# Scores, maxima and sums in one ring of three PSUM tiles, sums inverted on 128 partitions, the last pair scaled among the first MLP units

## The chip, the cores and the metric

The kernel runs on one core of one Trainium2 chip. The metric is the time of one execution on the device in microseconds (us), the median of several runs. The engines that compute are TensorE (PE, with its weight loads as PEld), VectorE (DVE), ScalarE (ACT) and GpSimd (POOL). SyncE (SP) issues nearly all transfers.

## What is computed

```python
# attention: q is averaged over pairs of positions first; 2 batches, 8 heads, 1152 positions, head size 64
scores = 1/sqrt(64) * matmul(q_pool, k.T)            # per head 576 x 1152
attn = exp(scores - max(scores))                     # maximum over the 1152 keys
attn = attn / (sum(attn) + 1e-9)
x = matmul(attn, v)                                  # -> 1152 tokens x 512
# two MLP layers, 512 -> 2048 -> 512
h = x @ w_in;  g = h * tanh(softplus(h));  x = g @ w_out        # layer 0 (Mish)
h = x @ w_in2; g = h if h > 0 else exp(h) - 1; out = g @ w_out2  # layer 1 (ELU)
```

The MLP weights come as 64-bit floats. Each block of them is rebuilt as a 32-bit float from its two words.

## The kernel before

**Pairs and steps.** The heads are taken in 8 pairs (two heads fill the 128 partitions). A pair has two halves of queries, c = 0 (256 queries) and c = 1 (320). Each half has 9 steps, one for each block of 128 keys, so a pair has 18 steps. In every step TensorE makes the transposed scores of that block (`qk`, L308: three products of high and low parts, and L310: a product that adds the row `top` with the negated maxima), and ACT takes the exponential (`exp`, L316) into the tile `pt`.

**Maxima.** The maxima have to be known before a pair's scores. So 14 "peaks" of the next pair (numbered 0 to 13) are worked in between: a product of queries and keys into the tile `M` (`peak_mm`, L254; the last two, for the queries that don't fill a block, at L260), and a reduction on DVE (`peak`, L268, L270, L272) into `stat`. After peak 5 and after peak 13 the maxima are negated (L280, L282), written to DRAM (`hopm`) and read back as a row (`top`, L291 and L296). Peaks 0 to 5 of the next pair stand at steps 5 to 10, peaks 6 to 13 at steps 12 to 17 and at steps 0 and 1 of their own pair. For pair 0, peaks 0 to 5 stand ahead of the first step and peaks 6 to 13 at steps 0 to 7.

**Output products and sums.** The products with v (`av`, L364, into the tile `C`) follow in groups: for c = 0 five key blocks at step 11 and four at step 15; for c = 1 five at step 2 of the next pair and four at step 6. POOL adds up part of the exponentials (`add`, L329) and TensorE finishes the sums over keys with a product of ones (`total`, L339, tile `T`) behind the group of four. Then DVE adds 1e-9 and inverts (`invert`, L347, L348; four rows of up to 160 numbers, repeated on 32 partitions each), the result goes through DRAM (`hop`, L350) and comes back spread over partitions (`rb`, L353). ACT copies the product out of `C` (`keep`, L372), DVE scales it 9 steps after the inversion (`scale`, L387), ACT and DVE split it into the high and low parts of the tokens (`token_high` L392 into `XH`, `token_low` L397 into `XL`).

**PSUM.** The 8 banks are: `M` one tile of two banks, `S` (scores) two tiles of two banks, `T` one bank, `C` one bank.

**What sets the order.** The code is emitted step by step in a fixed order that the table `todo` holds; each engine works through its own instructions in that order. In a step the peak's product comes first, then the scores, then `av`, ACT's work, DVE's, POOL's and SP's. Each pair also reads one half block of MLP weights (`Weights`): read at step 5 (SP, L97), and by its age in steps rescaled on ACT (4, L109), clamped on POOL (5, L113), shifted and merged with its words on DVE (7 and 8, L118, L123, L124), and split (9 and 10, L132, L135).

**MLP.** 96 units (2 layers, 48 each), one after another: TensorE makes `h` of unit u (L168), and the output products of unit u - 3 (L588).

## Time and profile before

| | |
|---|---|
| median of 3 runs | 771.13 us (766.66 to 772.33) |
| profiled execution, time | 777.13 us |
| profiled execution, span of its trace | 775.3 us |
| PE busy | 678.2 us (87%) |
| DVE busy | 456.5 us (59%) |
| ACT busy | 341.5 us (44%) |
| POOL busy | 233.8 us (30%) |

The attention stage ends at about 361 us and the MLP units begin there. The profile shows for each instruction its start, its duration and what it waited for; a busy TensorE need not be one at its peak, since its matmuls are pipelined and their ends modelled. "Granted clock" is the clock of TensorE, 1.00 for 2.4 GHz and 0.50 for 1.2 GHz.

### The profile page before, as it was taken

The page shows a single profiled execution, that of the slowest core. Times are in us where ns is not written, and L with a number is a line of the kernel's source. Part 1 is how long each engine was busy: PE and PEld are TensorE (multiplying, and loading weights), DVE is VectorE, ACT ScalarE, POOL GpSimd, SP SyncE. Part 2 cuts the span into 40 slices and gives each one's busy share as a digit, 9 for nine tenths or more (in the row PEclk, how much of TensorE's full clock was granted, in tenths as well). Part 3 has the DMA queues.
Part 4 walks back from the last instruction along what each step waited for, and adds up shares of the span by engine and source line. Part 5 has one row for each costly group of instructions (what it writes and reads, how often), then busy time and mean ns, then how long its engine had stood idle before and what let it go on. Part 6 is the DMA issues. An engine that isn't in the chain of part 4 may idle for free.

```text
span 775.3 us, 11575 instructions
## 1 busy us (share of the span) xinstructions
PE 678.2 (87%) x4616; PEld 569.5 (73%) x4616; DVE 456.5 (59%) x700; ACT 341.5 (44%) x678; POOL 233.8 (30%) x213
## 2 busy tenths in 40 slices
PE   2677878787778688699799999999999999999997
PEld 1455545455555455466799999999999989989996
DVE  4444464546463634624754666667778777998543
ACT  1333334243434333342543444444466666665442
POOL 3443545455553525343110112323322000110000
PEclk9998888798979878799899999999999999999999
DMA  2221121212131301011422322222212222230111
GB/s 91 89 68 32 41 97 37 92 42 94 35 101 36 101 8 51 25 37 42 165 82 82 109 81 70 95 82 82 82 55 82 82 82 82 83 109 1 41 42 41
DMA packets 43592, 53.30 MB, mean 69 GB/s; under 512 B 14033, under 2 KB 34449, under 8 KB 43537
## 3 DMA queue, kind: packets, MB, share of 16 engines
q1 hardware_dynamic: 43024, 51.83, 21.4%
q8 instruction: 36, 0.59, 0.3%
q10 hardware_dynamic: 512, 0.72, 0.3%
q14 instruction: 20, 0.16, 0.1%
HBM read 50.11 MB, written 2.43 MB: 68 GB/s over the span
## 4 chain that ended last, share of the span: by engine, by line
PE 78%; DVE 14%; ACT 3%; DMA 3%; issue 2%; SPq 1%
PE A L168 25%; PE B L588 21%; PE C L364 12%; DVE stat L268 6%; PE S L308 6%; PE C L588 5%; PE M L254 4%; PE T L339 3%; DVE inv L348 2%; PE S L310 2%; DVE wf L124 2%; ACT pt L316 2%; DVE wf L123 1%; DMA top<-hopm 1%; DVE stat L270 1%
## 5 line engine op out<-in xcount | busy, mean ns | idle before, releaser
L316 ACT ACTIVATE pt<-S 128x512 f32<-128x512 f32 (+1 forms) x144 | 92.6, 651 | 211.5 <-PE S L310 211.4
L268 DVE TENSOR_REDUCE stat<-M 128x2 f32<-128x768 f32 x96 | 91.1, 949 | 107.1 <-PE M L254 107.1
L168 PE MATMUL A<-XH,wh 128*128 128x384 f32 x384 | 129.7, 338 | 6.5 <-ACT g L543 5.9
L113 POOL TENSOR_SCALAR wf<-wf 128x512 f32<-128x512 f32 x64 | 42.8, 669 | 294.5 <-ACT wf L109 261.2
L168 PE MATMUL A<-XH,wl 128*128 128x384 f32 x384 | 129.6, 338 | 0.0
L168 PE MATMUL A<-XL,wh 128*128 128x384 f32 x384 | 129.4, 337 | 0.0
L254 PE MATMUL M<-KH,QH 64*128 64x384 f32 x192 | 49.8, 508 | 67.3 <-DVE stat L268 61.1
L364 PE MATMUL C<-pt,vr 128*64 128x320 f32 (+1 forms) x576 | 96.1, 490 | 0.5 <-ACT x L372 0.5
L254 PEld LDWEIGHTS M<-KH,QH 64*128 64x128 f32 x192 | 21.6, 217 | 91.3 <-DVE stat L268 74.7
L329 POOL TENSOR_TENSOR add<-pt 128x512 f32<-128x512 f32 (+1 forms) x32 | 45.1, 1410 | 122.0 <-ACT pt L316 121.9
L168 PEld LDWEIGHTS A<-XH,wh 128*128 128x128 f32 x384 | 72.6, 189 | 9.0 <-ACT g L543 6.2
L329 POOL TENSOR_TENSOR add<-add,pt 128x512 f32<-128x512 f32 (+1 forms) x48 | 73.3, 1541 | 16.7 <-ACT pt L316 16.6
L364 PEld LDWEIGHTS C<-pt,vr 128*64 128x64 f32 x576 | 46.4, 166 | 39.0 <-issue 19.9
L168 PEld LDWEIGHTS A<-XL,wh 128*128 128x128 f32 x384 | 72.7, 189 | 1.9
L168 PEld LDWEIGHTS A<-XH,wl 128*128 128x128 f32 x384 | 72.6, 189 | 0.0
L542 ACT ACTIVATE gh<-A 128x384 fp32r<-128x384 f32 x48 | 23.7, 494 | 81.5 <-PE A L168 81.5
L310 PE MATMUL S<-top,unit 64*128 64x320 f32 (+1 forms) x288 | 51.4, 339 | 6.8 <-DMA top<-hopm 6.8
L124 DVE SCALAR_TENSOR_TENSOR wf<-raw,wf 128x512 int32<-128x512 int32 x64 | 54.1, 845 | 2.2
L308 PE MATMUL S<-QH,KH 64*128 64x320 f32 (+1 forms) x288 | 53.5, 363 | 1.0 <-ACT pt L316 0.7
L545 DVE TENSOR_TENSOR gl<-g,gh 128x384 fp32r<-128x384 f32 x48 | 32.0, 668 | 35.8 <-ACT g L543 35.7
L588 PE MATMUL B<-gh,wh 128*128 128x384 f32 x155 | 52.3, 337 | 0.0
L588 PE MATMUL B<-gh,wl 128*128 128x384 f32 x155 | 52.2, 337 | 0.0
(88 smaller groups left out, 1369.7 us busy)
## 6 DMA issues: line engine op xcount, KB each, us to landing
raw<-in_moe_w_in_dram SPq DMA_DIRECT2D x32, 512.0 KB
raw<-in_moe_w_out_dram SPq DMA_DIRECT2D x32, 512.0 KB
vr<-in_v_dram SPq DMA_DIRECT2D x8, 576.0 KB
qr<-in_q_dram SPq DMA_DIRECT2D x7, 576.0 KB
kr<-in_k_dram SPq DMA_DIRECT2D x7, 576.0 KB
out_dram<-part SPq DMA_DIRECT2D x8, 256.0 KB
rb<-hop SPq DMA_DIRECT2D x16, 80.0 KB
rb<-hop SPq DMA_DIRECT2D x16, 64.0 KB
```

What stands on the lines that cost most here:

```text
L113: nc.gpsimd.tensor_scalar(self.f, self.f, HUGE, -HUGE, op0=ALU.min, op1=ALU.max)
L124: nc.vector.scalar_tensor_tensor(f, self.low, 29, f, op0=ALU.logical_shift_right, op1=ALU.bitwise_or)
L168: nc.tensor.matmul(pt[:, :TB], w[:, kk * P:(kk + 1) * P], x[:, kk, tk], start=(i == 0), stop=(i == len(terms) - 1))
L254: nc.tensor.matmul(pt[:, h, :KB], qh[n][half[h], t * P:(t + 1) * P], kh[n][half[h], j * KB:(j + 1) * KB], start=True, stop=True,)
L268: nc.vector.tensor_reduce(m[:, t, :, j], pt[:, :, :KB], axis=AX.X, op=ALU.max)
L308: nc.tensor.matmul(pt[:, h, :w], x[half[h], kk], y[half[h], cols], start=(i == 0), stop=False)
L310: nc.tensor.matmul(pt[:, h, :w], unit[half[h], :], tops[n % 2][half[h], cols], start=False, stop=True)
L316: nc.scalar.activation(pts[n, c][:, kt], sc.pop((n, c, kt))[:, :, :w], AF.Exp, scale=SCALE)
L329: nc.gpsimd.tensor_tensor(d, d if i is None else p[:, i], p[:, j], op=ALU.add)
L364: nc.tensor.matmul(acc[n, c][half[h], :w], vs[n][:, h, kt, :], pts[n, c][:, kt, h, :], start=(kt == 0), stop=(kt == KT - 1),)
L545: nc.vector.tensor_tensor(gl, g, gh, op=ALU.subtract)
L588: nc.tensor.matmul(pt, l, r, start=(first and i == 0), stop=(final and i == 2))
```

## The change

Five edits:

- **One ring.** Peaks, scores and sums take their PSUM tiles from one ring `S` of three tiles of two banks, in the order in which they are emitted. `C` gets two tiles instead of one, so that the output products can stay in PSUM until they are scaled.
- **Sums.** ACT copies the sums out of the ring (`spill`, one step after `total`); they go to DRAM and come back as one number or a few for each of 128 partitions (`tot`, 4 or 5 wide). DVE inverts these (`invert`, 4 steps after the copy), and they go to DRAM again (`pop`) and come back spread out (`rb`). `scale` follows 4 steps after `invert` (9 before), and reads the output products from `C`; the copy `keep` is left only for the last pair.
- **Last pair.** Its `invert`, `scale`, `token_high` and `token_low` stand in MLP units 1 to 7.
- **Weights** in the attention stage are read at step 12 instead of 5, so that their DVE work falls on steps 1, 2 and 4 of the next pair.
- **Pair 0.** Peaks 6 to 9 stand ahead of the first step too; 10 to 13 stand at steps 0 to 3.

```diff
-                pt = sc[n, e] = ps.tile([P, 2, 512], F32, tag="M", name="M", bufs=1)
+                pt = sc[n, e] = ps.tile([P, 2, 512], F32, tag="S", name="M", bufs=3)
...
-                pt = sc[n, c, kt] = ps.tile([P, 2, 512], F32, tag="S", name="S", bufs=2)
+                pt = sc[n, c, kt] = ps.tile([P, 2, 512], F32, tag="S", name="S", bufs=3)
...
-                pt = sums_[n, c] = ps.tile([P, 512], F32, tag="T", name="T", bufs=1)
+                pt = sums_[n, c] = ps.tile([P, 2, 512], F32, tag="S", name="T", bufs=3)[:, 0]
...
+            def by_four(hop):
+                return hop.rearrange("(g p) a -> g (p a)", g=4)
+
+            def spill(n, c):
+                w = cut[c][1] - cut[c][0]
+                r = ap.tile([P, 5 * D // 2], F32, tag="sum", name="sum")
+                nc.scalar.copy(r[:, :w // 2], sums_.pop((n, c))[:, :w // 2])
+                hop = dp.tile([P, w // D], F32, tag=f"hop{c}", name="hop")
+                nc.sync.dma_start(out=by_four(hop), in_=r.rearrange("(g p) w -> g p w", p=32)[:, 0, :w // 2])
+                pool, bufs = home(n)
+                r = tots[n, c] = pool.tile([P, w // D], F32, tag=f"tot{c}", name="tot", bufs=bufs)
+                nc.sync.dma_start(out=r, in_=hop)
+
             def invert(n, c):
-                w = (cut[c][1] - cut[c][0]) // 2
-                r = ap.tile([P, 5 * D // 2], F32, tag="inv", name="inv")
-                nc.vector.tensor_scalar(r[:, :w], sums_.pop((n, c))[:, :w], 1e-9, None, op0=ALU.add)
-                nc.vector.reciprocal(r[:, :w], r[:, :w])
-                hop = dp.tile([4, 5 * D // 2], F32, tag="hop", name="hop")
-                nc.sync.dma_start(out=hop[:, :w], in_=r.rearrange("(g p) w -> g p w", p=32)[:, 0, :w])
+                w = cut[c][1] - cut[c][0]
+                r = tots.pop((n, c))
+                nc.vector.tensor_scalar(r, r, 1e-9, None, op0=ALU.add)
+                nc.vector.reciprocal(r, r)
+                hop = dp.tile([P, w // D], F32, tag=f"pop{c}", name="pop")
+                nc.sync.dma_start(out=hop, in_=r)
...
-                    acc[n, c] = ps.tile([P, 512], F32, tag="C", name="C", bufs=1)
+                    acc[n, c] = ps.tile([P, 512], F32, tag="C", name="C", bufs=2)
...
             def scale(n, c):
-                rb, x = xs[n, c]["rb"], xs[n, c]["x"]
                 w = cut[c][1] - cut[c][0]
-                nc.vector.tensor_tensor(x[:, :w], x[:, :w], rb[:, :w], op=ALU.mult)
+                pool, bufs = home(n)
+                x = xs[n, c] = pool.tile([P, w], F32, tag=f"y{c}", name="y", bufs=1)
+                nc.vector.tensor_tensor(x, acc.pop((n, c))[:, :w], rbs.pop((n, c)), op=ALU.mult)
...
-                    at(u0 + KT + 6, "av", total, n, c)
-                    at(u0 + KT + 7, "dve", invert, n, c)
-                    at(u0 + KT + 7, "act", keep, n, c)
-                    at(u0 + KT + 16, "dve", scale, n, c)
-                    at(u0 + KT + 17, "act", token_high, n, c)
-                    at(u0 + KT + 18, "dve", token_low, n, c)
+                    t0 = u0 + KT + 6
+                    at(t0, "av", total, n, c)
+                    at(t0 + 1, "act", spill, n, c)
+                    if n < n_pairs - 1:
+                        at(t0 + 5, "dve", invert, n, c)
+                        at(t0 + 9, "dve", scale, n, c)
+                        at(t0 + 10, "act", token_high, n, c)
+                        at(t0 + 12, "dve", token_low, n, c)
+                    else:
+                        at(t0 + 1, "act", keep, n, c)
+                        for u, f in (1 + c, invert), (3 + 3 * c, scale), (3 + 3 * c, token_high), (4 + 3 * c, token_low):
+                            after.setdefault(u, []).append(lambda f=f, c=c: f(n_pairs - 1, c))
...
             for e in range(6, 14):
-                at(e - 6, "peak", peak_mm, 0, e)
-                at(e - 6, "dve", peak, 0, e)
+                if e < 10:
+                    peak_mm(0, e)
+                    peak(0, e)
+                else:
+                    at(e - 10, "peak", peak_mm, 0, e)
+                    at(e - 10, "dve", peak, 0, e)
...
-                if pieces and s % NS == 5:
+                if pieces and s % NS == 12:
```

Three places in the order of the instructions. First DVE, in one period of the loop before the change, from step 11 of a pair to step 1 of the next: `stat<-M` are reductions of peaks, `wf` and `wl` the weights, `inv` the inversion, `x<-x,rb` the scaling.

```order
L268 TENSOR_REDUCE stat<-M 128x2
L118 TENSOR_SCALAR wf<-wf 128x512
L268 TENSOR_REDUCE stat<-M 128x2
L123 SCALAR_TENSOR_TENSOR wf<-raw,wf 128x512
L124 SCALAR_TENSOR_TENSOR wf<-raw,wf 128x512
L268 TENSOR_REDUCE stat<-M 128x2 x2
L135 TENSOR_TENSOR wl<-wf,wh 128x512
L387 TENSOR_TENSOR x<-x,rb 128x320
L347 TENSOR_SCALAR inv<-T 128x128
L348 RECIPROCAL inv<-inv 128x128
L268 TENSOR_REDUCE stat<-M 128x2 x2
```

After the change, on the same engine, from step 1 of a pair to step 10 (`tot` are the sums, `y<-C,rb` the scaling):

```order
L120 TENSOR_SCALAR wf<-wf 128x512
L365 TENSOR_SCALAR tot<-tot 128x4
L366 RECIPROCAL tot<-tot 128x4
L125 SCALAR_TENSOR_TENSOR wf<-raw,wf 128x512
L126 SCALAR_TENSOR_TENSOR wf<-raw,wf 128x512
L137 TENSOR_TENSOR wl<-wf,wh 128x512
L269 TENSOR_REDUCE stat<-M 128x2
L406 TENSOR_TENSOR y<-C,rb 128x256
L269 TENSOR_REDUCE stat<-M 128x2 x3
L416 TENSOR_TENSOR XL<-y,XH 128x256
```

The weights' instructions have moved from between the reductions of peaks 6 to 11 to ahead of peak 0; the scaling of the first half stands between peaks 0 and 1.

Second SP, after the change, from the writing of the sums of the first half (`hop<-sum`) to the loads of the pair after next; `hopm` and `top` are the maxima.

```order
L357 DMA hop<-sum 4x128
L360 DMA tot<-hop 128x4
L287 DMA hopm<-neg 128x5
L292 DMA top_84<-hopm 1x256x1
L297 DMA top_84<-hopm 1x64x1
L292 DMA top_84<-hopm 1x256x1
L297 DMA top_84<-hopm 1x64x1
L368 DMA pop<-tot 128x4
L372 DMA rb<-pop 64x256 x2
```

Before, the corresponding part was this:

```order
L350 DMA hop<-inv 4x128
L353 DMA rb<-hop 64x2x128 x2
L286 DMA hopm<-neg 128x5
L291 DMA top_81<-hopm 1x256x1
L296 DMA top_81<-hopm 1x64x1
L291 DMA top_81<-hopm 1x256x1
L296 DMA top_81<-hopm 1x64x1
L97 DMA raw<-in_moe_w_out_dram 128x1024
```

The spread-out factors (`rb`) stood ahead of the maxima and now stand behind them.

Third ACT, after the change, from step 4 to the exponential of step 17: `pt<-S` are exponentials, `XH<-y` the high parts of scaled tokens, `sum<-T` the copy out of the ring.

```order
L317 ACTIVATE pt<-S 128x512 x4
L411 CAST XH<-y 128x256
L355 COPY sum<-T 128x160
L317 ACTIVATE pt<-S 128x512
L317 ACTIVATE pt<-S 128x640 x8
L411 CAST XH<-y 128x256
L411 CAST XH<-y 128x64
L355 COPY sum<-T 128x128
L111 ACTIVATE wf<-raw 128x512
L317 ACTIVATE pt<-S 128x640
```

Each copy of sums stands behind the exponential of the step after `total` and behind the casts of a half that has just been scaled. Before, no ACT instruction read the sums.

## Rows read from the trace of the kernel before

**Rows 1.** Busy time by stretches: us, engine (instructions), clock, DMA share, GB/s

```profile
50.00:95.00 45.00, 36.49 (x332) 24.21 (x331) 20.27 (x27) 16.48 (x30) 22.59 (x17) 0.85 0.19 59
480.00:580.00 100.00, 100.00 (x576) 99.70 (x575) 70.92 (x103) 47.94 (x100) 30.62 (x34) 1.00 0.27 85
```

**Rows 2.** Waits of TensorE: in total, times, longest

```profile
PE M L254 <- DVE stat L268: 61.1, 65, 2.8
```

**Rows 3.** Chain of waits at the start: start us, us, what

```profile
15.11 0.70 PE M L254 x2
...
17.03 1.40 DMA hopm<-neg
...
40.72 1.43 DMA hopm<-neg
...
44.47 2.78 DMA top<-hopm
...
50.38 3.14 PE C L364 x20
```

**Rows 4.** Chain of waits in pairs 2, 3 and 7 and at the end

```profile
134.53 3.72 PE C L364 x20
...
159.09 2.84 PE C L364 x20
165.21 2.31 PE C L364 x16
...
344.19 2.31 PE C L364 x20
...
359.33 1.27 PE T L339 x32
...
373.49 4.21 PE A L168 x12
```

**Rows 5.** Timeline, steps 13 to 15 of pair 2: start, us, engine, [idle before]

```profile
139.68 0.44 PE L254 MATMUL M<-KH,QH 64*128 64x384 f32 x2 [0.47 <-DVE stat L268]
...
139.96 0.31 PE L308 MATMUL S<-QH,KH 64*128 64x320 f32 x2
...
140.17 0.96 DVE L268 TENSOR_REDUCE stat<-M 128x2 f32<-128x768 f32 x1 [0.21 <-PE M L254]
...
140.75 0.71 ACT L316 ACTIVATE pt<-S 128x640 f32<-128x640 f32 x1 [0.79 <-PE S L310]
...
141.18 0.44 PE L254 MATMUL M<-KH,QH 64*128 64x384 f32 x2 [0.48 <-DVE stat L268]
...
142.17 1.91 DVE L124 SCALAR_TENSOR_TENSOR wf<-raw,wf 128x512 int32<-128x512 int32 x1
...
145.00 0.69 PE L254 MATMUL M<-KH,QH 64*128 64x384 f32 x2 [2.80 <-DVE stat L268]
```

**Rows 6.** Timeline of SP's queue: start, us to issue, what

```profile
158.76 0.33 SPq L286 DMA_DIRECT2D hopm<-neg  x1
...
163.46 0.58 SPq L97 DMA_DIRECT2D raw<-in_moe_w_out_dram  x1
...
178.35 1.72 SPq L291 DMA_DIRECT2D top<-hopm  x2
180.16 0.91 SPq L221 DMA_DIRECT2D vr<-in_v_dram  x1
```

**Rows 7.** Timeline, factors of the last pair's first half

```profile
354.72 0.52 SPq L350 DMA_DIRECT2D hop<-inv  x1
...
356.30 1.27 SPq L353 DMA_DIRECT2D rb<-hop  x2
...
359.65 0.43 DVE L387 TENSOR_TENSOR x<-x,rb 128x256 f32<-128x256 f32 x1 [3.95 <-DMA rb<-hop]
```

**Rows 8.** Groups of instructions: busy us, mean ns of one, idle before

```profile
L348 DVE RECIPROCAL inv<-inv 128x160 f32<-128x160 f32 x8 | 9.2, 1153 | 0.3
...
L372 ACT COPY x<-C 128x320 f32<-128x320 f32 x8 | 3.4, 421 | 4.1 <-PE C L364 4.1
```

31 lines of the change are left out of this document (18 added, 13 removed).

## The prediction

> **What bounds the kernel now.** I read the profile in four passes. First the busy time by stretches: in the MLP stage TensorE is busy all the time at the full clock, 100.00 of 100 us, while in the attention stage it is busy for 36.49 of 45 us at a mean granted clock of 0.85, that is about 0.3 of the time at 1.2 GHz and the rest at 2.4 GHz [rows 1]. So there is nothing to win after about 373 us, and the first 373 us have slack on every engine: DVE 20, ACT 16 and POOL 23 of those 45 us [rows 1]. Second, TensorE's waits: 61.1 us are waits of a peak product (L254) for the reduction of the peak before it [rows 2]. Third, the chain of waits, which gives the landmarks: the output products of step 11 start at 50.38 for pair 0 [rows 3] and at 344.19 for pair 7 [rows 4], so the seven pairs between take 42.0 us each; TensorE goes on without a break from 373.49 [rows 4]. Fourth, the timeline of steps 13 and 14 of pair 2: peak product at 139.68, reduction 140.17 to 141.13, next peak product 141.18. One tile for the peaks makes a step 1.50 us long, with 0.48 us of waiting in it. At the next step the reduction stands behind the weight words (1.91 us), and TensorE waits 2.80 us [rows 5].
>
> **The change part by part.** Times below are in us; P is a peak product, R its reduction, Q the scores of a step.
>
> *Ring of three.* P no longer waits for the R just before it; now Q of a step waits for the R of the step before, and P for the exponential of two steps before. Without its wait the step of 1.50 is 1.02; R with its gaps needs 1.0, and the loop R, Q, P, R about 1.1 where scores are 320 wide. I take 1.0 and 1.1 where nothing else holds the ring. The new price is the sums' tile. It sits in the same ring, and the copy that frees it stands on ACT behind the next step's exponential and one or two casts of a scaled half. From Q's start an exponential ends 1.50 later, 139.96 to 141.46 [rows 5], cast and copy add 0.42 each (both no longer than the copy of a 320-wide tile now [rows 8]; from below the cast may already be done, then it is the copy alone). Only then can the second peak product after the sums start. This is paid twice a pair.
>
> *Weight words* go from between the peaks to steps 1 to 4, where no peak is due: the 2.80 of [rows 5] goes. They lie under step 2's output products (2.84 [rows 4]) and cost ACT's cast a wait there; without that cover I count up to 1.7.
>
> *Sums* go through DRAM once more but are inverted 4 or 5 wide instead of 160: 1.15 of DVE goes [rows 8]. For the small inversions no row exists; between nothing and 0.33 each, I take 0.15. The scaling now comes 4 steps after the inversion instead of 9, in DVE's order ahead of a peak's R. If its factors are late, that R, and through the ring P, waits. From the issue of the write to the scaling the row says 354.72 to 359.65, 4.9, of which the write is 1.58 and the broadcasts 3.35 [rows 7]. The read of the sums is new: between 1.4 (a small write [rows 3]) and 3.4 (the broadcast); it has 4 steps and more to land, so I count it as covered.
>
> *One pair, added up from the start of step 2's output products (0).* The last peak is negated at about -0.3 and its write and four reads of the row of maxima hold SP until 163.46 - 159.09 = 4.4 [rows 6, 4]. Only then is the write of the inverted sums issued: +1.6 = 6.0, broadcasts +3.35 = 9.4, scaling 9.9, R of step 6 until 10.85. TensorE has meanwhile done step 2 (2.84), four steps of about 0.6 with the cast's wait of 1.7, step 6's products 2.31 and totals 1.27 (at 359.33 [rows 4]), together 10.6. So step 7's P starts at 10.9, its Q at 11.2, its exponential (256 wide) ends at 12.5, cast 12.95, copy 13.4, and step 8's P starts at 13.45. From there R by R, with a subtraction of 0.43 between, to the R of step 10, which ends at 17.3; the next output products start at 17.5. Second half: negated at 17.5, write 1.43 [rows 3], two reads 1.72, v 0.91 [rows 6], so SP issues the next write at 21.7. The 576 KB of v are ahead of it: landing between 23.3 (the row's 1.58) and 25 (5 us after the issue of v, like the write and broadcasts together [rows 7]); I take 24.0, in the middle. Broadcasts 27.35, scaling 27.85, R of step 15 28.8. TensorE is through with step 15 (five products 2.31, four steps of 1.1, four products 4/5 of that, totals 1.27 x 128/160) at 27.0 and waits 1.85. Q at 29.15, exponential 30.65, two casts and the copy 31.7; then steps 17, 0 and 1 with R's in a row (and 0.65 of subtractions) bring step 2's products at 35.9. A pair takes **36 instead of 42.0**. Bounds: 33.5 if the write does not wait behind v and copies are free when due, 40 if the clock is at 1.2 GHz for half of it.
>
> At this point the Trainium skill, "DMA: Bandwidth & Descriptors", section "Anatomy of one DMA", speaks against the change: it gives a fixed cost of about 2.0 us for each transfer (of the GpSimd path). The rows have 1.40 and 1.58 for small writes on SP's path [rows 3, 7]. By the page's figure the four writes on the two chains would add an estimated 2 us a pair, 38, and the time would be some 13 us higher; the sum stays with the rows.
>
> *Start.* Six peaks went one by one, product 0.70 and R 0.96, and were negated at 17.03 [rows 3, 5]. With R after R five gaps of about 0.75 go: negated at 13.2. From there to the landing I take what the later maxima take, 6.5 (40.72 to 44.47 + 2.78 [rows 3]), or a little less: 19.4. Four more peaks are reduced by about 18 under that transfer, the last four come one a step of 1.2, so the 14th is negated at about 24 instead of 40.72. Its rows land 6.5 later, at 30.6; TensorE, held by steps of 0.85 to 1.4 at half clock, comes to step 9 at about 31 and after three steps to the products of step 11 at **35.2 instead of 50.38**. Bounds 33.5 and 38.
>
> *End.* The last pair's scaling leaves the path between stages, but the first MLP weights still stand behind the copies and reads of sums on SP: they are issued about 1.6 earlier after the last totals than now (359.33 + 1.27 to 373.49 [rows 4]). Steps 11 to 17 of pair 7 gain 1.3. The last scaling lies under MLP units 1 to 7, where an exact price does not matter: first use is in unit 6, some 20 us later. In the two MLP layers nothing else changes.
>
> *Sum.* Products of step 11 of pair 0 at 35.2; first pair 33.5 (no previous half to scale); five pairs of 36; the seventh 31 (no peaks from step 5 on): 279.7 instead of 344.19, -64.5. With 1.3 and 1.6 it is **-67.4**. The profiled execution has span 775.3 and time 777.13, so it would become 709.7; it lies 6.0 above the median of the runs, 771.13, so I forecast the median at **704**.
>
> **The rivals.** (a) *Clock and ring eat part.* Period 39 to 42, because stretches after the two waits of TensorE are at 1.2 GHz, where five products take 3.72 instead of 2.31 [rows 4] and a step 0.4 more, or because P waits for exponentials nearly as long as it did for R. For it: clock 0.85 now [rows 1]. Against it: much of it would lie under the transfers. Three to six more a pair over 6.5 pairs: 722 to 743. (b) *Transfers are covered.* If the factors always land before the scaling, products and totals (11.5), 14 steps of 1.1 and 4 of 0.7 are 29.7: about 665 to 690. Against it: the four reads of maxima that stand ahead on SP [rows 6]. (c) *Slower.* TensorE stays at 1.2 GHz. Its work at full clock is about 28 a pair (11.5 of products and totals, 14 steps of 1.0, 4 of 0.6); the time passes 779, 1% above now, when a pair takes 47.5, so when 0.7 of it is at half clock, against 0.3 now; wholly at half clock a pair takes 56 and the kernel 835. The place would be steps 7 to 10 and 16 to 1, with a wait at each step. The Trainium skill, "TensorE: Matmul & The Clock Gate", section "A second HAM failure mode: psum-queue depth-cycling", has this rule: many short waits between groups that cycle through PSUM banks make the clock fall and rise again. By it (c) or (a) would hold; the trace agrees only so far that the attention stage with its waits is at 0.85 and the MLP stage at 1.00 [rows 1]. Against (c): the change takes waits away. (d) *Nothing gained:* the whole 67 is given back by periods of 46.4, with the transfers of both halves late by 10.4 together: 771.
>
> **How the numbers follow.** Forecast (a pair takes 34.5 to 38, 694 to 718): 0.58. (a) 0.20, (b) 0.13, (c) 0.04, (d) 0.05. The range leaves out the faster half of (b), the upper third of (a), (c) and (d), together about 0.2: 680 to 736. A measurement of this kernel tells about 1% from no change: faster 0.92, same 0.04, slower 0.04.
>
> **What would show it.** Right: the first output products near 35, the next pair's step 2 about 36 after step 2; waits of P for "stat" nearly gone, in their place waits for the copy of the sums and, on DVE, of the scaling for the broadcast (some 2 to 4 us twice a pair). Wrong: no such DVE waits (then b), granted clock under 0.75 in 50 to 300 us (then a or c), first output products after 40, or a gap before 373 that grows.

## The result

The changed kernel takes **729.87 us** (median of 4 runs, 728.98 to 732.69) where the kernel before takes 769.43 (4 runs, 766.66 to 772.33): ratio 0.949, 95% interval 0.944 to 0.954. The direction is as predicted and the time lies inside the range of 680 to 736, but the predicted time was 704: about 40 us came where about 67 were forecast. The measured time is the one that rival (a) gave. Of the runs further down, one of x4 (741.69 us) and one of x13 (716.83 us) fell in a slower state of the chip; they are left out of the ratios but not of the medians.

| | before | after |
|---|---|---|
| profiled execution, time | 777.13 us | 730.59 us |
| its span | 775.3 us | 728.8 us |
| PE busy | 678.2 us (87%) | 668.0 us (92%) |
| DVE busy | 456.5 us (59%) | 431.4 us (59%) |
| ACT busy | 341.5 us (44%) | 337.8 us (46%) |
| POOL busy | 233.8 us (30%) | 229.6 us (32%) |

The same stretches as in [rows 1], of after (the columns are span of the stretch, then busy us and instructions of PE, PEld, DVE, ACT and POOL, the granted clock, DMA share and GB/s):

```profile
50.00:95.00 45.00, 37.90 (x345) 24.40 (x339) 21.74 (x34) 18.82 (x38) 22.72 (x17) 0.85 0.22 60
480.00:580.00 100.00, 100.00 (x541) 95.81 (x540) 77.73 (x126) 58.28 (x121) 24.95 (x28) 1.00 0.25 80
```

The MLP is as it was. In the attention stage TensorE is a little busier, and its clock is still 0.85. The waits, which answer to [rows 2] (us in total, times, longest):

```profile
DVE y L406 <- DMA rb<-pop: 58.4, 15, 6.6
...
PE S L309 <- DVE stat L269: 31.3, 33, 3.9
...
PE M L255 <- DVE stat L269: 6.2, 14, 0.9
...
PE S L309 <- ACT sum L355: 0.6, 1, 0.6
```

The 61.1 us that a peak's product waited for the reduction before it are down to 6.2. In their place the scores wait 31.3 us for a reduction, and DVE stands 58.4 us in front of its scalings until their factors `rb` have landed. The landmarks that answer to [rows 3] and [rows 4] (timeline of TensorE; the first output products of step 11 of pairs 2 and 3, and those of steps 2 and 6 between them):

```profile
106.83 2.38 PE L382 MATMUL C<-pt,vr 128*64 128x256 f32 x20
...
128.63 3.86 PE L382 MATMUL C<-pt,vr 128*64 128x320 f32 x20
...
137.32 4.07 PE L382 MATMUL C<-pt,vr 128*64 128x320 f32 x16
...
148.10 1.08 PE L382 MATMUL C<-pt,vr 128*64 128x256 f32 x8
```

Over the eight pairs these products start at 32.16, 66.62, 106.83, 148.10, 185.04, 226.63, 267.69 and 300.53. A pair in the middle (a "steady pair" below: pairs 1 to 5, each from its step 11 to that of the next) takes (267.69 - 66.62) / 5 = 40.2 us, not 36; before the change the same five take 42.6. Most of the difference to 36 begins in one place, shown here for pair 2 (the timeline from step 15 on: start, us, engine, [idle before]):

```profile
110.14 0.95 SPq L222 DMA_DIRECT2D vr<-in_v_dram  x1
...
111.18 0.42 SPq L368 DMA_DIRECT2D pop<-tot  x1
...
115.33 1.14 SPq L372 DMA_DIRECT2D rb<-pop  x2
...
116.40 0.44 PE L255 MATMUL M<-KH,QH 64*128 64x384 f32 x2
116.56 1.26 SPq L217 DMA_DIRECT2D qr<-in_q_dram  x1
117.87 0.42 SPq L210 DMA_DIRECT2D kr<-in_k_dram  x1
118.35 0.42 SPq L99 DMA_DIRECT2D raw<-in_moe_w_in_dram  x1
118.92 0.49 DVE L406 TENSOR_TENSOR y<-C,rb 128x320 f32<-128x320 f32 x1 [6.23 <-DMA rb<-pop]
119.33 1.81 DVE L269 TENSOR_REDUCE stat<-M 128x2 f32<-128x768 f32 x2
...
120.33 0.63 PE L309 MATMUL S<-QH,KH 64*128 64x320 f32 x2 [3.48 <-DVE stat L269]
```

Read it from the top. The read of v (576 KB) is issued at 110.14, and 1.04 us later, on the same queue, the write `pop` of the inverted sums. The broadcasts `rb` may only be issued when `pop` has landed, at 115.33: 4.15 us. They have landed at 118.92. DVE has stood still for 6.23 us, with the reduction of the peak of 116.40 behind the scaling, and TensorE has waited 3.48 us for that reduction. What the clock makes of it, in stretches of 2 us (columns as above):

```profile
118.00:120.00 2.00, 0.00 (x0) 0.00 (x0) 1.08 (x2) 0.00 (x0) 0.00 (x0) 1.00 0.73 200
120.00:122.00 2.00, 1.67 (x10) 1.30 (x10) 1.14 (x2) 0.19 (x1) 0.00 (x0) 0.59 1.00 401
...
128.00:130.00 2.00, 2.00 (x14) 1.17 (x12) 1.97 (x3) 2.00 (x4) 1.27 (x1) 0.50 0.04 1
130.00:132.00 2.00, 2.00 (x14) 0.94 (x12) 0.40 (x1) 1.06 (x4) 0.00 (x0) 0.85 0.09 1
...
138.00:140.00 2.00, 2.00 (x12) 0.84 (x10) 1.03 (x2) 0.03 (x1) 2.00 (x3) 0.50 0.03 8
```

TensorE does nothing from 118 to 120, and from then until about 130 it has 1.2 GHz. So the products of step 2 last 3.86 us instead of the 2.84 of [rows 4]. The clock is then full again, and falls a second time, from about 137 to 141, over the products of step 6 (4.07 us instead of 2.31). What stands in front of that second fall are two short waits, not one for `rb`:

```profile
135.00 0.44 PE L255 MATMUL M<-KH,QH 64*128 64x384 f32 x2 [0.40 <-ACT pt L317]
136.63 0.39 PE L309 MATMUL S<-QH,KH 64*128 64x256 f32 x2 [1.20 <-DVE stat L269]
```

Pair 2 is not every pair. The five steady ones, each from its step 11 on (the mean granted clock is that of the whole pair):

| pair from | us | `pop` to `rb`, second half | wait of the scores behind it | clock |
|---|---|---|---|---|
| 66.62 | 40.2 | 3.47 | 2.38 | 0.83 |
| 106.83 | 41.3 | 4.15 | 3.48 | 0.83 |
| 148.10 | 36.9 | 3.61 | 2.41 | 0.91 |
| 185.04 | 41.6 | 3.87 | 3.88 | 0.84 |
| 226.63 | 41.1 | 3.77 | 3.51 | 0.83 |

```profile
79.00 0.41 PE L309 MATMUL S<-QH,KH 64*128 64x320 f32 x2 [2.38 <-DVE stat L269]
...
160.52 0.42 PE L309 MATMUL S<-QH,KH 64*128 64x320 f32 x2 [2.41 <-DVE stat L269]
```

The pair from 148.10 has the same wait as the one from 66.62, and also the short waits at step 6, but its clock falls only once, from about 161 to 168. It takes 3.3 us less, and is the one that comes near the forecast 36. So the wait alone doesn't say how long the clock stays down.

### The profile page after: what moved, and what is told of

Read it like the earlier page. It is cut to its first block, busy times and chain, and to the rows that moved or that the text cites. A ratio compares the mean times of both kernels' runs of the same rounds, so it can differ in the third digit from the quotient of the medians.

```text
span 728.8 us, 11613 instructions
## 1 busy us (share of the span) xinstructions
PE 668.0 (92%) x4616; PEld 559.9 (77%) x4616; DVE 431.4 (59%) x700; ACT 337.8 (46%) x680; POOL 229.6 (32%) x213
## 4 chain that ended last, share of the span: by engine, by line
PE 54%; DMA 1%; ACT 0%; DVE 0%; issue 0%; SPq 0%
PE A L170 27%; PE B L617 22%; PE C L617 5%; DMA raw<-in_moe_w_out_dram 1%; DVE part L642 0%; DMA hop<-sum 0%; ACT L571 0%; ACT g L572 0%; SPq L99 0%; ACT gh L571 0%; SPq L360 0%; ACT wf L111 0%
## 5 line engine op out<-in xcount | busy, mean ns | idle before, releaser
L309 PE MATMUL S<-QH,KH 64*128 64x320 f32 (+1 forms) x288 | 58.4, 400 | 34.6 <-DVE stat L269 31.3
L382 PE MATMUL C<-pt,vr 128*64 128x320 f32 (+1 forms) x576 | 88.6, 459 | 0.0
L309 PEld LDWEIGHTS S<-QH,KH 64*128 64x128 f32 x288 | 30.7, 208 | 62.2 <-DVE stat L269 43.0
L382 PEld LDWEIGHTS C<-pt,vr 128*64 128x64 f32 x576 | 42.9, 152 | 35.2 <-issue 17.2
L330 POOL TENSOR_TENSOR add<-add,pt 128x512 f32<-128x512 f32 (+1 forms) x48 | 69.7, 1473 | 0.0
L137 DVE TENSOR_TENSOR wl<-wf,wh 128x512 fp32r<-128x512 f32 x64 | 49.4, 772 | 25.2 <-ACT wh L134 25.2
L255 PE MATMUL M<-KH,QH 64*128 64x384 f32 x192 | 42.5, 438 | 14.8 <-DVE stat L269 6.2
L111 ACT ACTIVATE wf<-raw 128x512 f32<-128x512 f32 x64 | 43.1, 674 | 21.8 <-DMA raw<-in_moe_w_in_dram 13.7
L126 DVE SCALAR_TENSOR_TENSOR wf<-raw,wf 128x512 int32<-128x512 int32 x64 | 51.8, 809 | 2.2
L617 PE MATMUL B<-gl,wh 128*128 128x384 f32 x155 | 52.3, 337 | 0.0
```

Source lines behind the costliest of these rows:

```text
L111: nc.scalar.activation(self.f, self.top.bitcast(F32), AF.Identity, scale=2.0 ** -112)
L126: nc.vector.scalar_tensor_tensor(f, self.low, 29, f, op0=ALU.logical_shift_right, op1=ALU.bitwise_or)
L137: eng.tensor_tensor(self.l, self.f, self.h, op=ALU.subtract)
L255: nc.tensor.matmul(pt[:, h, :KB], qh[n][half[h], t * P:(t + 1) * P], kh[n][half[h], j * KB:(j + 1) * KB], start=True, stop=True,)
L309: nc.tensor.matmul(pt[:, h, :w], x[half[h], kk], y[half[h], cols], start=(i == 0), stop=False)
L330: nc.gpsimd.tensor_tensor(d, d if i is None else p[:, i], p[:, j], op=ALU.add)
```

## The experiments

Two questions were open. Is it the queue (what stands ahead of `pop`, and behind `rb`) that makes a pair 40.2 us, and does the clock merely follow the wait? Or do the clock and the ring themselves set the pair, so that moving transfers gives nothing (rival C below, which is rival (a) of the prediction)? All runs are given as ratios to the kernel before, measured beside them on the same chip, so that they compare with the 0.949 of the change. The lengths of pairs and the clocks are those of one profiled execution of each.

### One suspect at a time

**v three steps later** (x1), so that `pop` is issued ahead of it:

```diff
-                    at(s0 - 8, "sp", load_v, n)
+                    at(s0 - 5, "sp", load_v, n)
```

> The changed kernel with one edit: v of the next pair is loaded at step 13 instead of step 10, so that its 576 KB no longer stand between the maxima and the inverted sums of the half c = 1. In the changed kernel that write takes 4.15 us from its issue to the broadcasts (111.18 to 115.33), the scaling starts at 118.92, and TensorE, which is through with step 15 and its totals at 116.4, waits 3.48 us for the reduction behind it; then the clock is 1.2 GHz for some 10 us. Theory W (the period is set by this chain of transfers, and the fall of the clock follows from the wait it causes): the write lands 1.5 us after its issue, the issue is 0.95 us earlier, the wait at step 16 is under 1 us in pairs 1 to 6, and steps 16 to 6 run at the full clock: 6 pairs by 3.3 + up to 3.9 us, 690 to 705 us, granted clock over 0.92 between 50 and 260 us. Rival C (the wait shrinks, but the clock falls anyway, because TensorE has too little to do in these steps): 6 x 3.3 = 20 us, about 710, clock as before 0.85. Rival N (the wait only moves to the next late transfer): within 4 us of 730.

Measured: 711.8 us, ratio 0.919 (0.912 to 0.926), steady pairs 37.65 us. In the queue of pair 2 nothing large is left ahead of `pop`:

```profile
105.06 1.00 SPq L368 DMA_DIRECT2D pop<-tot  x1
107.97 1.14 SPq L372 DMA_DIRECT2D rb<-pop  x2
...
110.25 0.43 SPq L99 DMA_DIRECT2D raw<-in_moe_w_in_dram  x1
110.78 1.05 SPq L222 DMA_DIRECT2D vr<-in_v_dram  x1
```

`pop` to `rb` is 2.91 instead of 4.15 us (2.59 to 2.95 over the pairs, where it was 3.47 to 4.15), and the waits of the scores for a reduction fall from 31.3 to 14.3 us, while those of the peaks' products rise from 6.2 to 18.0. One number in the table of steps is worth 0.03 of the time. The granted clock from 50 to 265 us rises from 0.85 to 0.90 with it. Neither theory is met: `pop` does not come down to 1.5 us and the waits behind the scaling stay at 1.4 to 2.5 us in four of the five steady pairs, so the time is not theory W's 690 to 705 but near rival C's 710, while the clock rises, which rival C excluded.

**The wait filled** (x2): twelve products of 512 columns go into the unused bank of the totals' tile behind the first half's totals of pairs 1 to 6. They add work whose result nothing uses.

```diff
+                if c == 0 and 0 < n < n_pairs - 1:
+                    for _ in range(12):
+                        nc.tensor.matmul(both[:, 1], kh[n][:, :P], kh[n][:, :512], start=True, stop=True)
```

> The changed kernel with 12 more products of 128x512 on TensorE behind the totals of the half c = 0 in pairs 1 to 6, into the unused half of the tile of sums; nothing reads them. They take about 12 x 0.22 = 2.6 us at full clock, in the place where TensorE otherwise waits 3.5 us for the reduction behind the scaling, so they delay nothing there. Theory W (the idle wait makes the clock fall, and the fall costs 1.2 us in steps 16 to 1, 1.0 at step 2 and 1.6 at step 6): the clock stays at 2.4 GHz behind it and a pair gets shorter by up to 3.9 us, 6 x 3.9 = 23 us, 707 to 720 us. Rival C (the clock falls for the low use of TensorE in all these steps): no gain, 728 to 735, and the granted clock between 50 and 260 us stays at 0.85.

Measured: 725.09 us, 0.9365 (0.931 to 0.942), steady pairs 38.4. More work in less time. The transfers are as late as before (DVE waits up to 7.7 us for `rb`), but TensorE's idle time in front of the scores is shorter (17.1 us of waits for a reduction in all, not 31.3) and the clock is 0.94 from 50 to 265 us. In pair 2 only one stretch of 2 us is left that is wholly at half clock:

```profile
118.00:120.00 2.00, 0.43 (x6) 0.43 (x8) 1.84 (x3) 0.00 (x0) 0.00 (x0) 1.00 0.94 355
120.00:122.00 2.00, 1.64 (x14) 1.13 (x14) 1.46 (x3) 1.31 (x4) 0.00 (x0) 0.84 0.97 361
122.00:124.00 2.00, 2.00 (x12) 1.24 (x10) 0.83 (x3) 0.75 (x2) 0.00 (x0) 0.50 0.25 87
124.00:126.00 2.00, 2.00 (x23) 1.59 (x21) 1.35 (x5) 1.31 (x3) 2.00 (x2) 0.81 0.04 1
```

The pair is 1.8 us shorter although it does more. This lies between theory W (707 to 720 us) and rival C (728 to 735, clock still 0.85). At least part of the half clock follows the idle time, then, and does not come with the ring's steps as such.

**Words read at step 5 again** (x3):

```diff
-                if pieces and s % NS == 12:
+                if pieces and s % NS == 5:
```

> The changed kernel with the weights read at step 5 again, so that their words stand on DVE between the reductions of peaks 7 to 9 as before the change. Theory W (steps 11 to 15 are not what the period hangs on, since TensorE waits at step 16 for the transfers anyway): the words' delay of 2 to 3 us lies in that wait, and steps 2 to 6 lose the wait for the cast of the weights: 725 to 735 us. Rival D (the move of the words took the wait of 2.8 us away once a pair, and it comes back): 7 x 2.3 = 16 us more, about 746.

Measured: 726.02 us, 0.938 (0.9325 to 0.943): not slower than the changed kernel, rather 0.01 faster. From step 11 to step 15 the pair now takes about 10.5 us instead of 6.7, since the reductions stand behind the words again (theory D was right so far), but the pair as a whole is shorter, 38.1 us. What was saved between the peaks was spent on the transfers that were late anyway. And the words at step 12 stand on SP behind `rb`, which the next group shows to be a cost.

**Peaks 6 to 13 of pair 0 at steps 0 to 7 again** (x4; `peak_mm` and `peak` of these eight by `at(e - 6, ...)` as before):

> The changed kernel with peaks 6 to 13 of pair 0 at steps 0 to 7 again. The output products of step 11 of pair 0 start at 32.2 us in the changed kernel and at 50.4 before. If the earlier peaks carry the gain of the start, the 14th peak comes four steps of about 1.4 us later and with it the second maxima: 5 to 7 us more, 735 to 737. If the ring alone carries it, within 2 us of 730.

Measured: 737.25 us, 0.949 (0.941 to 0.956). The first output products start at 39.92 us instead of 32.16, so the start costs 7.8 us as such. The total cannot be told from the changed kernel, because the six periods behind it are 1.2 us shorter in that run (38.0 against 39.3). The profiled run of x4 is also the fastest of its four, 1% below their median. A part of what makes its periods shorter is in its trace: of its five steady pairs two have a clock of 0.83 and take about 40.2 us, three have 0.91 and take 38.2, 38.3 and 38.5. In the changed kernel only one of five has 0.91. The code of these pairs is the same in both. So under the same code a pair takes some 2 us more or less with the clock that it gets, and this helped to hide what the later start costs.

### The way through DVE and the way through ACT

**Scalings two steps later** (x9), with no transfer moved, so that the reductions stand ahead of the scaling:

```diff
-                        at(t0 + 9, "dve", scale, n, c)
-                        at(t0 + 10, "act", token_high, n, c)
-                        at(t0 + 12, "dve", token_low, n, c)
+                        at(t0 + 11, "dve", scale, n, c)
+                        at(t0 + 12, "act", token_high, n, c)
+                        at(t0 + 13, "dve", token_low, n, c)
```

> The changed kernel with the scaling of each half (all pairs but the last) two steps later (step 11 of its totals' count instead of 9, token_high 12 instead of 10, token_low 13 instead of 12). No transfer moves and no operation is added: only the place at which VectorE stands still for rb. In the changed kernel the scalings wait 58.4 us in 15 stops, and the products behind them 31.3 us for VectorE's maxima. Theory W (the stop of VectorE in front of the maxima is the loss, and TensorE's half clock follows from it): most of the stops go, steady pairs fall from 40.2 to 36 to 37 us, the granted clock of the pairs rises from 0.85 to above 0.9, the time is 0.91 to 0.925 of the kernel before (about 703 to 712 us for 770). Rival C (the clock falls anyway, by the shape of the steps, and the wait lies under something else): pairs above 38.5 us, ratio 0.935 to 0.95. Rival N (the wait only moves, to the next half's slot of the ring or to the products of the output that wait for the second tile of C): 0.945 to 0.955.

Measured: 733.48 us, 0.953 (0.950 to 0.957), pairs 40.85. Theory W failed in this form: DVE's waits for `rb` fall from 58.4 to 24.4 us, the scores' waits for a reduction only from 31.3 to 25.8, and nothing is gained; the ratio is in rival N's range. A new wait appears on ACT (timeline of ACT, pair 2):

```profile
117.38 0.26 ACT L355 COPY sum<-T 128x128 f32<-128x128 f32 x1
125.25 0.66 ACT L111 ACTIVATE wf<-raw 128x512 f32<-128x512 f32 x1 [7.61 <-DMA raw<-in_moe_w_in_dram]
125.81 0.69 ACT L317 ACTIVATE pt<-S 128x640 f32<-128x640 f32 x1
```

ACT stands 7.61 us in front of the rescaling of the weight words, and the exponentials stand behind it; the scores now wait 17.9 us for exponentials, in six stops. The words were read on the same queue, behind `pop`, `rb`, q and k (the SP rows of the result). In the changed kernel that wait was only 1.19 us at the same place, because TensorE was already held up by the other. So there are two ways from one late queue to TensorE, and to take one away uncovers the other.

**v at step 4 of its own pair, scalings later** (x10), and **the inversions one step earlier too** (x12):

```diff
-                    at(s0 - 8, "sp", load_v, n)
+                    at(s0 + 4, "sp", load_v, n)
...
-                        at(t0 + 5, "dve", invert, n, c)
+                        at(t0 + 4, "dve", invert, n, c)
```

> The scalings two steps later as in x9_scale_late, and v of a pair read at step 4 of the pair itself (its products with v begin at step 10) instead of step 8 of the pair before, so that the write of the inverted sums no longer stands behind its 576 KB. Theory W: x9 has taken the stops away, what is late behind v no longer reaches TensorE, so this gives 0 to 1 us a pair more: ratio 0.905 to 0.925, and the landing of the second half's rb after its pop falls from 7.7 us to about 5.5 us. If the transfer behind v still sets the pair in x9, this one is 2 us a pair better than x9 (0.015 in the ratio). Rival C: equal to x9 within 0.005.

> As x10_scale_late_v4, and the inversion of each half one step earlier (step 4 of its totals' count instead of 5). If anything of the sums' way still reaches TensorE, this is better than x10 by up to 1 us a pair (0.01); theory W expects the same as x10 within 0.005, since the stops are gone; if the totals have not landed at step 4, VectorE stops at the inversion instead and it is worse by up to 1 us a pair.

Measured: x10 725.17 us, 0.941 (0.937 to 0.944), pairs 40.1; x12 720.1 us, 0.934 (0.931 to 0.938), pairs 39.45. Both are above what theory W expected of them, though x10 is 0.012 better than x9 and x12 another 0.006: in x10 ACT still waits 4.67 to 5.92 us for the words in every middle pair. With the scaling later and the words still at the end of the queue, even the gain of x1 is not reached.

**v and the words at step 4, nothing else** (x13; the words are converted at the same steps as in the changed kernel), and **all four edits** (x14: v, words, scalings later, inversions earlier):

```diff
-                if pieces and s % NS == 12:
+                if pieces and s % NS == 4:
                     going.append(Weights(*pieces.pop(0)))
+                    going[-1].age = -8
```

> The changed kernel with two transfers moved on the sync queue and nothing else: v of a pair is read at step 4 of the pair itself, and the 512 KB words of a weight piece are read at step 4 instead of 12 (converted at the same steps as before). In the changed kernel and in the two runs before, pop stands behind v (4.15 us to land), rb behind pop, and q, k and the words behind rb: ScalarE then stops for the words (7.6 us in the run with the later scaling, 13.7 us in 5 stops in the changed kernel), with exponentials behind it. Theory W2 (the queue of the second half is the bound in two ways, through rb in front of VectorE's maxima and through the words in front of ScalarE's exponentials; taking one away leaves the other, which is why the later scaling gained nothing): ScalarE's waits for raw vanish, steady pairs come to 36 to 37.5 us, ratio 0.900 to 0.918, better than x1_v_late (0.919). Rival C (the half clock after step 15 sets the pair whatever waits): as x10_scale_late_v4, 0.935 to 0.945.

> As x13_v4_raw4, and the scalings two steps later and the inversions one step earlier as in x12. Theory W2: now both ways are clear, TensorE's waits for VectorE's maxima in front of S fall from 31.3 us to under 10 us, the granted clock of the pairs is above 0.93, steady pairs 34 to 36 us, ratio 0.89 to 0.905, and at least 0.01 better than x13. If only the words were still in the way, equal to x13 within 0.005. Rival C: 0.925 to 0.94.

Measured: x13 706.96 us, 0.917 (0.911 to 0.922), pairs 36.1; x14 **691.23 us** (687.68 to 694.41), 0.896 (0.891 to 0.901), pairs 33.5. This is what theory W2 expected and rival C excluded: the first is at the upper end of its band (and cannot be told from x1 by the intervals), the second in the middle of it, with pairs a little shorter still than the 34 to 36 us expected. One expectation was missed: the scores' waits for a reduction are 11.3 us, where under 10 were expected. The four edits change only when things are issued, and leave the ring and the products alone; they give 0.053 of the time. SP's queue of x14 in pair 2 (start, us to issue, what):

```profile
99.78 0.34 SPq L368 DMA_DIRECT2D pop<-tot  x1
102.03 1.14 SPq L372 DMA_DIRECT2D rb<-pop  x2
103.26 0.54 SPq L287 DMA_DIRECT2D hopm<-neg  x1
```

And DVE in the same pair, a reduction and the scaling behind it:

```profile
107.93 0.96 DVE L269 TENSOR_REDUCE stat<-M 128x2 f32<-128x768 f32 x1 [3.13 <-PE M L255]
108.81 0.48 DVE L406 TENSOR_TENSOR y<-C,rb 128x320 f32<-128x320 f32 x1
```

With the inversion one step earlier `pop` stands ahead of `hopm` and its reads too, and lands in 2.25 us (1.41 to 2.25 over the second halves). The scaling at 108.81 waits for nothing. The whole kernel's waits (compare the result):

```profile
DVE tot L365 <- DMA tot<-hop: 13.7, 8, 4.0
...
PE S L309 <- DVE stat L269: 11.3, 19, 1.2
...
PE M L255 <- DVE stat L269: 8.6, 19, 0.9
DVE y L406 <- DMA rb<-pop: 5.5, 2, 5.0
```

The granted clock from 50 to 265 us is 0.97. This version beats both kernels.

The earlier inversion has a price of its own: DVE now stands 13.7 us for the sums (`tot`), 4.2 in the changed kernel. The one slow pair of x14 (from 163.38, 36.7 us at 0.91 among others of 31.7 to 33.8) shows where that can lead. DVE waits there 1.81 us for `tot`, the merge of the weight words behind it also takes 1.70 us (0.7 in the other steady pairs), ACT's cast of them stands in front of an exponential, and TensorE waits for that exponential:

```profile
186.81 0.69 PE L255 MATMUL M<-KH,QH 64*128 64x384 f32 x2 [2.31 <-ACT pt L317]
```

| kernel | steady pair, us | waits of S for a reduction, us | clock, 50 to 265 us | ratio |
|---|---|---|---|---|
| the change | 40.2 | 31.3 | 0.85 | 0.949 |
| x9, scalings later | 40.85 | 25.8 | 0.88 | 0.953 |
| x10, and v at step 4 | 40.1 | 13.8 | 0.88 | 0.941 |
| x12, and inversions earlier | 39.45 | 11.8 | 0.90 | 0.934 |
| x14, and words at step 4 | 33.5 | 11.3 | 0.97 | 0.896 |
| x1, v three steps later alone | 37.65 | 14.3 | 0.90 | 0.919 |
| x13, v and words at step 4 | 36.1 | 13.7 | 0.94 | 0.917 |

The last step from x12 to x14 takes no wait from the reductions (11.8 to 11.3); it takes ACT's wait for the words away (25.2 us in six stops from 60 to 300 us in x12, none in x14).

**What a wait costs with its clock.** x13 holds the same pair in two conditions. These are its pairs from step 11 to step 11 (columns as in the result):

```profile
99.00:132.00 33.00, 28.29 (x307) 18.93 (x307) 19.99 (x30) 15.26 (x31) 20.77 (x15) 1.00 0.27 80
...
170.00:210.00 40.00, 34.00 (x307) 21.96 (x303) 19.10 (x29) 15.29 (x30) 20.34 (x15) 0.83 0.24 67
```

The longest wait of TensorE in the short pair, behind step 15 (timeline):

```profile
109.56 0.44 PE L255 MATMUL M<-KH,QH 64*128 64x384 f32 x2 [0.97 <-DVE stat L269]
```

and in the longer pair:

```profile
182.11 0.44 PE L255 MATMUL M<-KH,QH 64*128 64x384 f32 x2 [2.79 <-DVE stat L269]
```

The same products (307 records in both) take 33.3 us (98.97 to 132.25) in the one and 40.4 (169.70 to 210.06) in the other. The wait differs by 1.8 us; the pair differs by 7.1. In the first the clock stays at 1.00, in the second its mean is 0.83, with two stretches at 0.50 (about 183 to 193 and 200 to 203 us). That is 13.7 us at half clock; if TensorE's work were what everything waited for in all of it, it would cost at most half of that, 6.8 us. How much of the other 5.3 us it does cost is not shown. The pair before the longer one (from 132.25, 37.45 us) has a wait of only 1.11 us at this place, hardly more than the 0.97, and still a clock of 0.86:

```profile
143.00 0.44 PE L255 MATMUL M<-KH,QH 64*128 64x384 f32 x2 [1.11 <-DVE stat L269]
```

So here too a longer wait goes with a lower clock, but a short one does not keep it up.

### The ring and the end

**Without the ring** (x6 on the changed kernel, x15 on x14):

```diff
-                pt = sc[n, e] = ps.tile([P, 2, 512], F32, tag="S", name="M", bufs=3)
+                pt = sc[n, e] = ps.tile([P, 2, 512], F32, tag="M", name="M", bufs=1)
...
-                pt = sc[n, c, kt] = ps.tile([P, 2, 512], F32, tag="S", name="S", bufs=3)
+                pt = sc[n, c, kt] = ps.tile([P, 2, 512], F32, tag="S", name="S", bufs=2)
...
-                pt = sums_[n, c] = ps.tile([P, 2, 512], F32, tag="S", name="T", bufs=3)[:, 0]
+                pt = sums_[n, c] = ps.tile([P, 512], F32, tag="T", name="T", bufs=1)
...
-                    acc[n, c] = ps.tile([P, 512], F32, tag="C", name="C", bufs=2)
+                    acc[n, c] = ps.tile([P, 512], F32, tag="C", name="C", bufs=1)
...
+                    at(t0 + 1, "act", keep, n, c)
```

> The changed kernel without its ring: the maxima have one tile of two banks, the scores two, the totals one bank, the output one bank that ScalarE copies out (keep for every pair), as before; the order of the start, the sums on 128 partitions, the words' step and the end stay as changed. The products of the maxima waited 61.1 us for VectorE in the kernel before. If the ring is what took those waits away (the prediction's step for the steady pairs), nearly all of the steady gain goes and only the end and part of the start stay: 0.975 to 1.0 of the kernel before, steady pairs 41 to 43 us, M waiting for stat 45 to 65 us. If the shorter way of the sums and the moved words carry the gain, ratio 0.945 to 0.96.

> x14_v4_raw4_sl_inv (both transfers moved, scalings later, inversions earlier) without the ring: one tile for the maxima, two for the scores, one bank each for the totals and the output, which ScalarE copies out, as in the kernel before. It asks what the ring is worth once the transfers are out of the way. x6_no_ring against the changed kernel gave the ring 0.025 of the time. Theory W2 (the ring's gain was partly eaten by the transfers of the second half): here it is worth more, 0.03 to 0.05, ratio 0.925 to 0.945, TensorE's products of the maxima wait 40 to 65 us for VectorE. If the transfers were all that held the kernel and the ring adds only its start, ratio 0.905 to 0.92.

Measured: x6 750.56 us, 0.974 (0.970 to 0.979), steady pairs 41.4, first output products at 40.78; x15 717.6 us, 0.927 (0.922 to 0.933), pairs 36.1, first products at 41.37. The peaks wait for their one tile again. The waits of TensorE in x6 (total, times, longest):

```profile
PE M L255 <- DVE stat L269: 68.8, 72, 4.5
```

and in x15:

```profile
PE M L255 <- DVE stat L269: 50.0, 69, 2.0
```

The ring is worth 0.025 (19 us) in the changed kernel and 0.031 (24 us) with the transfers out of the way; the first output products are late again by 8.6 and 8.7 us in both runs. x6 came out just under the 0.975 that the ring's theory expected at least, and its peaks wait more than the expected 45 to 65 us. But "nearly all of the steady gain" did not go: of the 2.4 us that a steady pair gained by the change (42.6 to 40.2) the ring carries only 1.2 (41.4 to 40.2). In x14 it carries 2.6 (36.1 to 33.5). The waits of [rows 2] for the one tile are gone in the changed kernel, but most of what they cost in the steady pairs came back as the waits for `rb`.

**The last pair scaled inside the attention** (x5):

```diff
-                    if n < n_pairs - 1:
+                    if True:
```

> The changed kernel with the last pair inverted, scaled and split inside the attention again, at the steps of the other pairs, instead of among the first units of the MLP. The prediction gave the end 1.3 and 1.6 us. It should show from the end of the last totals to the first product of A: 10.8 us in the changed kernel, 12.9 us in the kernel before; here 12.5 to 15 us, because the scaling waits for rb before the MLP's first words and products are issued. The whole: 2 to 4 us above the changed kernel, ratio 0.951 to 0.957, which the interval may not tell from it. If the end gained nothing by this, 10 to 11.5 us and 0.946 to 0.952.

Measured: 743.37 us, 0.961 (0.956 to 0.966), 0.012 (9 us) above the changed kernel, more than twice what was expected. From the end of the last totals to the first product of `A` it is 13.96 us, as expected; but in the changed kernel that is only 0.78. The 10.8 of the expectation is the time to a later point there, the end of a break of 3.51 us that x5 does not have. So x5 waits 14.0 us where the changed kernel waits 0.78 and 3.51: 9.7 more, and the two spans stand 9.5 apart. The first product of the MLP waits:

```profile
PE A L170 <- DVE y L406: 14.0, 1, 14.0
```

The releaser is the scaling itself and not the tokens that it leads to; unit 0 does not use the last pair's tokens. The reason that fits is PSUM: with the change the scaling reads the output products there, so the attention's PSUM stays taken until `rb` has landed, and the MLP's `A` tiles can't be had. It seems to be held as a whole: in the built program the first `A` tile takes bank 0, and the output products have banks 6 and 7. The copy `keep`, which the change leaves for the last pair, would free it: in the changed kernel the first `A` products start at 316.72, released by that copy 0.78 us after the last totals. A run of x5 with the copy put back was not made, so this is argued and not shown.

## Why the prediction was right, and where it was 26 us off

Against the profiled execution the sum was -67.4 us; the span fell by 775.3 - 728.8 = 46.5. Term by term:

| term | before | forecast | measured | difference to forecast |
|---|---|---|---|---|
| first output products, pair 0 | 50.3 | 35.2 | 32.16 | -3.0 |
| first pair | 41.9 | 33.5 | 34.5 | +1.0 |
| five steady pairs | 5 x 42.6 | 5 x 36 | 5 x 40.2 | +21.1 |
| seventh | 39.0 | 31 | 32.8 | +1.8 |
| from there to the end of the span | 431.2 | 428.2 (431.1 - 2.9) | 428.3 | +0.1 |

The differences sum to 21.0, and the two spans stand 20.9 apart. (In the medians 26 us are missing; 6.0 of the forecast was the distance of the profiled execution to its median, which for the changed kernel is only 0.7.) So one term carries the miss. The same table says where the gain came from: 18 of the 46.5 us are the start, only 12 the five steady pairs, from which 33 were forecast. The start gained 3 us more than forecast, which made up for a part of the miss.

- **Ring: right as a mechanism.** Peaks wait 6.2 instead of 61.1 us, the steps shorten, and steps 11 to 15 take 6.7 us as forecast. x6 and x15 show its value.
- **The write behind v: the first step that failed.** `pop` behind v was priced at 2.3 us (21.7 to 24.0), in the middle between two rows. It is 3.47 to 4.15 us in the steady pairs, in all of them beyond the later of the two bounds that the prediction kept (25, which is 3.3). With v later it is 2.91 in pair 2 (x1), and with `hopm` and its reads behind it as well 2.25 (x14). TensorE then waits 2.38 to 3.88 us instead of 1.85. On the mean of the five pairs the scores behind that wait come 1.5 us later than forecast, a third of the 4.3 us that a pair is too long.
- **"Much of it would lie under the transfers": the second failure.** Rival (a) was held at 0.20 by this sentence. The other two thirds come behind the wait. In pair 2 the clock falls after the wait, when TensorE is what most waits for: from the scores behind the wait to the products of step 2 it takes 8.3 us instead of 6.75, and from there to the next products of step 11 19.5 instead of 17.5. With the 1.85 by which those scores come later (13.5 us after the products of step 11 instead of 11.65) the excess of that pair is whole: 1.85 + 1.55 + 1.97 = 5.4 (41.3 against 35.9). The products of steps 2 and 6 alone, 3.86 and 4.07 us instead of 2.84 and 2.31, are 2.8 of it, more than the late landing. On the mean of the five pairs the three parts are 1.5, 1.4 and 1.4. The second fall of the clock, at step 6, is not behind the wait for `rb`, and the pair from 148.10, with a wait of 2.41 and without that fall, is over the forecast by 1.0 us only. x2 shows that part of the half clock goes when the idle time at that wait is filled, x14 that nearly all of it goes when the transfers are out of the way; what decides how long it lasts in a given pair is not shown.
- **The copy of the sums: priced, and not there.** The prediction let the second peak after the totals wait for the copy, twice a pair. All waits for it together are 0.6 us. The tiles are not handed out in turn; the built program's order (name and first bank) is

```
C6 M2 S0 M4 S2 M0 S4 M2 S0 T4 M2 S0 M2 S0 M4 S2
```

  While the totals hold tile 4, peaks and scores work with the other two, so each waits for the one just before it, and the copy is long done when tile 4 is due. The error was on the safe side, and hid part of the two above.
- **Words: sized right where they were, not where they went.** The 2.80 of [rows 5] went, but the words' read now stands last in the SP queue. That was priced at up to 1.7 us; it was 1.2 to 1.7 in the changed kernel, and 4.7 to 8.6 in the steady pairs when the scaling no longer covered it (x9, x10). x3 shows that the move as a whole gained nothing.
- **Sums on 128 partitions: right.** The inversions last 0.16 to 0.19 us (0.15 was taken; one 128x5 addition took 1.00), and the new read of the sums is covered: DVE waits for it once, for 1.2 us, between 40 and 300 us.
- **Start: under-sized.** Peak 5 was negated at 11.91 instead of the 13.2 forecast, and peak 13 at 23.16 (24).
- **End: right in size,** for the two reasons given: from the last totals to where TensorE goes on without a break it is 10.8 us instead of 12.9 (1.6 were forecast, 2.1 came), and steps 11 to 17 of pair 7 with their totals take 15.4 instead of 16.4 (1.3 were forecast, 1.0 came). That the copy `keep` may be what makes it possible had not been seen (x5).
- **Rival (c)** was right on the clock and wrong on the sum: TensorE does fall to 1.2 GHz, for about 10 us behind that wait, but the waits taken away outweigh it. **Rival (b)**, factors that land before the scaling, is nearly the case of x14 (5.5 us of waits for `rb` in the whole kernel): a pair takes 33.5 us, not the 29.7 worked out for it, and the kernel 691, just above its 665 to 690.

Two rules of the Trainium skill bear on this. "DMA: Bandwidth & Descriptors", section "Queues, rings and completion order", says that on each DMA engine descriptors are consumed in the order of their ring; by that a small write issued on a queue behind a large read comes behind it on each engine that both use, and the 4.15 us against 2.91 and 2.25 agree. The fixed cost of about 2.0 us that the same page's "Anatomy of one DMA" gives for the GpSimd path, and that the prediction set against its rows of SP's path, lies within what `pop` takes in x14 with no large read ahead (1.41 to 2.25 in the second halves), and is about half of what it takes behind v.

"TensorE: Matmul & The Clock Gate", section "HAM oscillation — how this bites in real kernels", describes a kernel in which every wait for a transfer makes the clock fall, once per tile. Here the clock falls behind the wait at `rb` in every steady pair (0.50 from 122 to 130 us in pair 2) and in four of the five once more at step 6, and with the wait gone it is 0.97 (x14). The other rule, "A second HAM failure mode: psum-queue depth-cycling", which the prediction weighed, is borne out in small part only: x14 cycles through the same ring, with 38 waits of at most 1.2 us of scores and peaks for reductions, and its clock from 50 to 265 us is 0.97; but it falls three times there, two of them behind waits of 1.0 to 1.2 us.

**Left open:** why the clock falls once in some pairs and twice in others of the same code, how much of the 7.1 us in x13 the clock takes by itself, and whether a later inversion would take x14's waits for `tot` away without bringing those for `rb` back.

## What to carry to other kernels

When a wait is moved from a tile to a transfer, cost the queue and not the transfer: list what is issued ahead of the small write on its queue and what large read stands behind its successor, because both reach the path, and taking one away may only uncover the other. A large load belongs in the place of the queue where nothing small follows soon, even if its data is needed only a half turn later. A wait of TensorE is to be priced with the half clock that can follow it: in pair 2 a wait of 3.48 us was followed by steps that took 1.55 us more than forecast and by products of step 2 that took another 1.0 more, an estimate of 2.6 us in all.

## What the runs showed of the hardware

- A write of 5 numbers on each of 128 partitions landed in 1.41 to 2.25 us with no large read and no reads of the maxima just ahead of it on SP's queue (x14), in 2.59 to 2.95 behind two reads of the row of maxima (x1), and in 3.47 to 4.15 us when v's 576 KB had been issued 1.04 us before it (the change); from issue to the issue that waits for it, steady pairs.
- Twelve added products of 512 columns a pair, in a place where TensorE stood idle, made the kernel faster, 0.9365 against 0.949, with a clock of 0.94 instead of 0.85 from 50 to 265 us.
- The same 307 products of a pair took 33.3 us at a clock of 1.00 and 40.4 at 0.83, in one execution, after waits of 0.97 and 2.79 us.
- Under the same code and after waits of 2.38 and 2.41 us, two pairs of the changed kernel had clocks of 0.83 and 0.91 and took 40.2 and 36.9 us.
